# Moving the late attention loads and probability writes to another engine's queue, and re-ordering additions in a fused attention and feed-forward kernel

## The chip, the cores and the metric

The kernel runs on 1 core of a Trainium2 chip. Its engines each run one instruction stream in order: TensorE (PE, matmuls; PEld is its weight load), VectorE (DVE), ScalarE (ACT), GpSimd (POOL) and SyncE (SP, which here only issues DMA transfers). POOL and ACT can issue DMAs too. The metric is the time of one execution on the device, in microseconds (us); lower is better. "KB" is 1024 bytes.

## The reference

Attention with 4 batches, 8 heads, 768 positions and a head size of 64, in which a position sees 8 global keys and a local band of 96, with a slope per head for the distance; then a feed-forward layer 512 -> 2048 -> 512 with a leaky ReLU over the 3072 rows.

```python
scores = scale * np.matmul(q, k.transpose(0, 1, 3, 2))
is_global = pos[None, :] < int(n_global)
is_local = (rel >= 0) & (rel < int(n_local))
scores = scores - slopes[:, None, None] * dist
scores = np.where(is_global | is_local, scores, -1000000000.0)
a = np.exp(scores - np.max(scores, axis=-1, keepdims=True))
attn = np.matmul(a / (np.sum(a, axis=-1, keepdims=True) + 1e-09), v)
h = x @ w_in            # x: attn as 3072 rows of 512
return np.maximum(0.01 * h, h) @ w_out
```

All in float32, which the kernel reaches with products of a high and a low part (three matmuls for one).

## The kernel before, in words

**Attention** is cut into 48 units (24 blocks of 128 rows, two groups of four heads). A unit u goes through: loads of queries, keys and values (`qs`, `kr` in `load_qk`, L158 to L173; `vr` in `load_v`, L175 to L183), scores on PE (L200), biased scores and row maxima on DVE (`biased`, L214, into the buffer `pr`), exponentials on ACT (L229), sums and scaling on DVE (`sums`, L249 to L256), a transposition in 32x32 blocks on DVE (L259) that is completed by a trip through DRAM (`move`, L232: one DMA `via<-pr` out, L239, then four DMAs `pt<-via` back, L241), and at last the product with the values (`attn_v`, L333 and L345). There are two `pr` buffers, so unit u+2 can write its biased scores only once the `via` of unit u has left.

**Feed-forward** runs as 80 steps j over chunks of 3, 3, 3, 3 and 2 blocks of rows (`order`, L463): each step is 12 matmuls into `ps_h` (L1155 to L1157, `hidden`) and, for the step before, 9 or 6 into `ps_o` (L1176 to L1178, `project`). The attention of later rows is put between these steps: up to unit 21 by `event`, one unit at a time (two of them at j = 32 and 33, L836), and from unit PAIRS = 22 on by `visit`, two units at a time, at the steps listed in `VISITS` (L26). A visit t takes the values' product of units t-4 and t-3, the scores of t and t+1, loads for t+2 and t+3 (queries, keys) and for t-2 and t-1 (values). Its exponentials and sums are spread over the next two steps through the list `behind`. All of the loads, the `via` writes, the `pt` reads and the output rows are issued by SP, in one order; POOL issues only the results of attention to DRAM (`xd<-xo`, L363) and one reload (L576). SP's order in a visit is: `qs`, `kr`, `kr`, `vr`, `vr`, then `via` and four `pt` of the first unit, `via` and four `pt` of the second. A `pt` read waits until its `via` has landed.

**Strassen-like stage.** The last 10 blocks of rows (two super-blocks of 4 and 6) are computed after step 79 in 16 pairs of hidden columns, with 7 products a pair instead of 8 (`strassen`, L674). `prepare(n)` (L590), called at the steps j = 80 + n from n = -10 on, frees the attention's buffers, loads the blocks of x and makes their differences and splits; `make_sum` (L549) makes sums of weights on POOL, except `s3` of the pairs n + 2 < 8, which DVE makes (L756, L806). `prepare_next(i)` (L639) loads and subtracts blocks of the second super-block, in the pairs of the first. `add` (L701) reads a product from PSUM on DVE and then lets out the waiting low-part subtractions (`flush`, L509); `pin` and `keep_in_program_order` keep an instruction at its place in the order of the text; unpinned ones (the DMAs of `move`) are placed by the compiler's scheduler.

Of the kernel before, what the change touches and what calls it, by code (L numbers as in the profile page):

```python
# [18 lines left out]
P = 128  # L19
# [3 lines left out]
PAIRS = 22  # L23
HT = 384
SUPERS = [4, 6]
VISITS = [37, 39, 41, 43, 45, 48, 50, 52, 55, 57, 59, 62, 64, 67, 69]  # L26
RELOAD = 50
TB = 32
G = 8
# [3 lines left out]
KC = G + WIN + HALF  # L33
# [20 lines left out]
def fast_path(ctx, tc, qp, kp, vp, wi, wo, nvec, weights, nmall, out, B, H, S):  # L54
    nc = tc.nc
# [48 lines left out]
    def pin(ins):  # L104

        if pinned[0]:
            tc.keep_in_program_order(ins)
# [24 lines left out]
    def where(u):  # L132
        s, uu = divmod(u, NU)
        return s, uu, s % NB
# [23 lines left out]
    qs = {}  # L158

    def load_qk(u):  # L160
        s, uu, i = where(u)
        if uu == 0:
            qs[s] = raw.tile([P, 2 * NU, P], F32, tag="qkr", name="qs")
            pin(nc.sync.dma_start(out=qs[s], in_=qp[s]))
        k = raw.tile([P, 2, 2, KC], F32, name="kr")
        if i:
            pin(nc.sync.dma_start(out=k, in_=kp[s, uu]))
        elif u < BY_DVE:
            pin(nc.sync.dma_start(out=k[:, :, :, KC - P:], in_=kp[s, uu][:, :, :, KC - P:]))
        else:  # L170
            kd, ks = (x.rearrange("p a f (s x) -> p (a f s) x", s=2) for x in (k, kp[s, uu]))
            nc.sync.dma_start(out=kd[:, :, (KC - P) // 2:], in_=ks[:, :, (KC - P) // 2:])
        units[u] = dict(q=qs[s][:, 2 * uu:2 * uu + 2], k=k)  # L173

    def load_v(u):  # L175
        s, uu, i = where(u)
        if u > PAIRS and u % 4 == (PAIRS + 3) % 4:
            v = att.tile([P, 5, 2, D], F32, tag="pt", name="vr", bufs=1)
        else:
            v = raw.tile([P, 5, 2, D], F32, name="vr", bufs=3)  # L180
        g0 = 0 if i else 3
        pin(nc.sync.dma_start(out=v[:, g0:], in_=vp[s, uu][:, g0:]))
        units[u]["v"] = v  # L183

    def tall(u):
# [46 lines left out]
    def move(u, pr):  # L232


        pt = raw.tile([P, 4 * KW], F32, tag="stage", name="pt", bufs=STAGES)
        src, dst = blocks(u, pr), blocks(u, pt)
        n = src.shape[-1]
        via = dram.tile([4, TB, 4, 2 * n], F32, tag="via", name="via", bufs=3)
        nc.sync.dma_start(out=via.rearrange("b p c x -> (b p) c x"), in_=src.rearrange("p c j x -> p c (j x)"))  # L239
        for c in range(4):  # L240
            nc.sync.dma_start(out=dst[c * TB:(c + 1) * TB].rearrange("p b j x -> p b (j x)"),  # L241
                              in_=via[:, :, c].rearrange("b p x -> p b x"))
        units[u]["pt"] = pt
# [129 lines left out]
    def event(t, conv=()):  # L373
# [23 lines left out]
        if t + 2 < NUNIT:  # L397
            load_qk(t + 2)
# [107 lines left out]
    NP = NF // 2  # L506
    lows = []

    def flush():  # L509
        while lows:  # L510
            lows.pop(0)()
# [4 lines left out]
    late, here, blocks_x, dd = {}, {}, [{}, {}], {}  # L516

    def half_of(n):
        return SUPERS[n // NP] * P // 2

    def value(x):
        return x[1].bitcast(F32)
# [7 lines left out]
    def split_x(x, v=None):  # L530
        v = value(x) if v is None else v
        pin(nc.scalar.copy(out=x[0], in_=v))
        low(x[1], v, x[0])

    def spare():
        return pools["mem"].tile([P, 2, HT], F32, tag="diff", name="diff", bufs=2)

    def minus(out, in0, in1):
        pin(nc.vector.tensor_tensor(out=out, in0=in0, in1=in1, op=ALU.subtract))
        return out  # L540
# [8 lines left out]
    def make_sum(n, k, eng=nc.gpsimd):  # L549

        if n >= len(SUPERS) * NP:
            return
        b = blocks_of(n % NP)
        a11, a12, a21, a22 = ([x.bitcast(F32) for x in b[k]] for k in ("a11", "a12", "a21", "a22"))
        terms = dict(s1=(a21[0], (ALU.add, a22[0]), (ALU.add, a21[1]), (ALU.add, a22[1])),
                     s2=(here["s1"], (ALU.subtract, a11[0]), (ALU.subtract, a11[1])),
                     s3=(a11[0], (ALU.subtract, a21[0]), (ALU.add, a11[1]), (ALU.subtract, a21[1])),
                     s4=(a12[0], (ALU.subtract, here["s2"]), (ALU.add, a12[1])))[k]
        acc_ = terms[0]
        for op, t in terms[1:]:  # L560
            pin(eng.tensor_tensor(out=here[k], in0=acc_, in1=t, op=op))  # L561
            acc_ = here[k]
# [27 lines left out]
    def prepare(n):  # L590

        xa = blocks_x[0]
        if n == -10:
            early.close()
            pools["mem"] = mem = phase.enter_context(tc.tile_pool(name="late", bufs=1, side="right", reuse_waits="tile"))
            pools["ps"] = phase.enter_context(tc.tile_pool(name="ps_q", bufs=1, space=bass.MemoryType.PSUM, side="right", reuse_waits="tile"))
            late["x"] = x = mem.tile([P, 5 * 4 * HT], F32R, name="x")
            for m, k in enumerate(("b11", "t2", "b21", "t3", "t1", "t4", "b22")):
                cut(0, k, x, m * 2 * SUPERS[0] * P)
            for m, k in enumerate(("b21", "t3", "t1", "t4", "b22")):  # L600
                cut(1, k, x, m * 2 * SUPERS[1] * P)
            for k, to in (("b12", "t3"), ("b11", "b11"), ("b22", "b22"), ("b21", "b21")):
                load_x(0, k, value(xa[to]))
            for k in ("s1", "s2", "s3", "s4"):
                late[k] = [mem.tile([P, 2, P], F32R, name=k + x_) for x_ in "hl"]
                here[k] = mem.tile([P, 2, P], F32, name=k)
            for k in ("s1", "s2", "s3", "s4"):
                make_sum(0, k)
            band_holds(tc, fl, nvec, nmall)
        elif n == -9:  # L610
            band_holds_everywhere(tc, fl, pools["ps"].tile([P, HT], F32, tag="ps_p", name="ps_f")[0:1, 0:1], flag)
        elif n == -8:
            late["d1"] = minus(spare()[:, :, :half_of(0)], value(xa["t3"]), value(xa["b11"]))
            late["d2"] = minus(spare()[:, :, :half_of(0)], value(xa["b22"]), late["d1"])
        elif n == -7:
            split_x(xa["b11"])
            split_x(xa["t1"], late["d1"])
        elif n == -6:
            split_sum(0, "s2")
            split_sum(0, "s3")  # L620
            split_x(xa["t2"], late["d2"])
        elif n == -5:
            split_sum(0, "s1")
            split_sum(0, "s4")
            flush()
            for k in ("s1", "s2", "s3", "s4"):
                make_sum(1, k)
            late["d4"] = minus(spare()[:, :, :half_of(0)], late["d2"], value(xa["b21"]))
        elif n == -4:
            split_x(xa["t4"], late["d4"])  # L630
        elif n == -3:
            late["d3"] = minus(spare()[:, :, :half_of(0)], value(xa["b22"]), value(xa["t3"]))
            split_x(xa["b21"])
        elif n == -2:
            split_x(xa["t3"], late["d3"])
        elif n == -1:
            split_x(xa["b22"])
# [36 lines left out]
    def strassen():  # L674
# [26 lines left out]
        def add(name, in0, ps, op=ALU.add):  # L701
            t = (in0 if name is None else
                 (ffn if name == "t" else mem).tile([P, HT], F32, name=name, **(dict(bufs=2) if name == "u2" else {}))[:, :ps.shape[-1]])
            pin(nc.vector.tensor_tensor(out=t, in0=in0, in1=ps, op=op))  # L704
            flush()
            return t
# [30 lines left out]
        for n in range(last + 1):  # L737
# [14 lines left out]
            i, ht = n % NP, half_of(n)  # L752
            b = blocks_of(i)
            x, y = ((lambda bank=bank: bank()[:, :ht]) for bank in (banks[::-1] if n % 2 else banks))
            change = n == NP - 1
            sums_by = nc.vector if n + 2 < NP else nc.gpsimd  # L756
            gs = {}
            ps = x()
            product(n, b["a11"], "b11", ps)
# [32 lines left out]
            if change:  # L792
                fetch_next("t1")
            c22 = add("t", u3, ps)
            if change:
                split_x(blocks_x[1]["b21"])
            split_sum(n + 1, "s1")
# [5 lines left out]
            c21 = add(None, u3, ps2, ALU.subtract)  # L803
            for k in ("s1", "s2"):
                make_sum(n + 2, k)
            make_sum(n + 2, "s3", sums_by)  # L806
            if n == last - 1:
                gs[1, 0] = halves(c21, ht)
            gs[1, 1] = halves(c22, ht)
# [8 lines left out]
                gs[1, 0] = halves(c21, ht)  # L818
            if change:
                split_x(blocks_x[1]["t1"])  # L820
            if n < NP:
                prepare_next(i)
            rest = lambda gs=gs, c12=c12, ht=ht: gs.update({(0, 1): halves(c12, ht)})
            behind_(12)
            todo = [(lambda m=m, n=n, gs=gs: second(n, gs, m)) for m in range(2 * SUPERS[n // NP])]
# [6 lines left out]
    ev_at = {}  # L832
    for c in (1, 2):
        events = range(NU * first_step[c] + 2, NU * first_step[c + 1] + 2)
        ev_at.update(spread(events, range(1, half) if c == 1 else [24, 25, 27, 28, 30, 31]))
    ev_at.update({32: [20], 33: [21]})  # L836
    ev_at.update({j: [t] for j, t in zip(VISITS, range(PAIRS, NUNIT + 4, 2))})

    for t in range(2):
        load_qk(t)  # L840
# [424 lines left out]
```

## Time and profile before

| | us |
|---|---|
| median of 3 runs | 713.54 (710.51 to 715.38) |
| the profiled execution, its own time | 708.05 |
| span of the profiled execution | 706.5 |
| PE busy | 637.2 (90%) |
| DVE busy | 480.2 (68%) |
| ACT busy | 298.5 (42%) |
| POOL busy | 161.6 (23%) |
| mean granted TensorE clock | 0.965 |

The span runs from the first to the last instruction of the program. Busy shares are means over stages: the attention events take the first 206 us or so, the visits lie between 223 and 434 us, `prepare` between 435 and 467 us, the Strassen-like stage from 467 us on, its first super-block until about 573 us. A row of a timeline gives start, duration, engine, line, operation, tiles and, in brackets, how long the engine had been idle and what ended it. "q" behind an engine's name is its sequencer, as in SPq, which issues DMAs.

### The profile page before, as it was taken

The numbers are of one execution on the slowest core, as the hardware profiler recorded it, in microseconds if no ns is written. First come the engines' busy times: TensorE is split into PE (matmuls) and PEld (weight loads), VectorE is DVE, ScalarE is ACT, GpSimd is POOL, SyncE is SP. The second block draws the span as 40 slices with busy tenths as digits, with TensorE's granted clock in tenths as the row PEclk, the third lists the DMA queues.
The fourth block names the chain that finished last, engine by engine and source line by source line (L and its number), as shares of the span: only waits on it lengthen the run. The fifth ranks groups of instructions, "written<-read, shape, count | busy, mean of one in ns | idle before, by whom it ended". The sixth has DMA issues, their size and how long they took to land.

```text
span 706.5 us, 15386 instructions
## 1 busy us (share of the span) xinstructions
PE 637.2 (90%) x5836; PEld 554.7 (79%) x5836; DVE 480.2 (68%) x1319; ACT 298.5 (42%) x876; POOL 161.6 (23%) x220
## 2 busy tenths in 40 slices
PE   5799999999979978987969796989978979999996
PEld 4589898888868867876859785877857868888985
DVE  6988989866664765655665461687977876666743
ACT  6977745554433444443434341433233333223211
POOL 4213100000000000010000013343543655544500
PEclk9899999999999999988999898999999999999999
DMA  8975534226674557678666673020100300000002
GB/s 270 333 271 191 188 134 149 90 84 206 213 230 117 174 176 223 209 260 219 227 210 197 204 239 110 28 96 24 46 23 24 113 31 30 1 1 0 1 2 93
DMA packets 60321, 95.98 MB, mean 136 GB/s; under 512 B 10448, under 2 KB 33744, under 8 KB 60240
## 3 DMA queue, kind: packets, MB, share of 16 engines
q1 hardware_dynamic: 58800, 90.99, 39.8%
q0 software_dynamic: 1296, 3.67, 1.6%
q8 instruction: 48, 0.79, 0.5%
q14 instruction: 33, 0.27, 0.1%
q10 hardware_dynamic: 144, 0.26, 0.1%
HBM read 71.44 MB, written 23.46 MB: 134 GB/s over the span
## 4 chain that ended last, share of the span: by engine, by line
PE 59%; DVE 17%; DMA 10%; ACT 6%; issue 4%; SPq 2%; POOL 1%; ACTq 0%; DVEq 0%; POOLq 0%
PE ps_p L684 9%; PE ps_o L1178 7%; PE ps_o L1176 6%; PE ps_o L1177 6%; PE ps_h L1155 6%; PE ps_h L1157 5%; PE ps_h L1156 5%; DMA via<-pr 5%; DMA vr<-in_vp_dram 4%; PE ps_q L1177 2%; PE ps_q L1176 2%; PE ps_q L1178 2%; PE ps_v L345 2%; SPq L241 2%; DVE s L561 2%
## 5 line engine op out<-in xcount | busy, mean ns | idle before, releaser
L1176 PE MATMUL ps_o<-woh,gh 128*128 128x512 f32 x288 | 114.2, 396 | 3.7 <-ACT gh L1165 3.0
L1178 PE MATMUL ps_o<-woh,gl 128*128 128x512 f32 x288 | 114.5, 398 | 0.1
L1177 PE MATMUL ps_o<-wol,gh 128*128 128x512 f32 x288 | 113.5, 394 | 0.0
L1155 PE MATMUL ps_h<-xh,wih 128*128 128x384 f32 (+1 forms) x320 | 108.3, 338 | 0.1
L1156 PE MATMUL ps_h<-xl,wih 128*128 128x384 f32 (+1 forms) x320 | 104.5, 326 | 0.0
L1157 PE MATMUL ps_h<-xh,wil 128*128 128x384 f32 (+1 forms) x320 | 104.3, 326 | 0.0
L363 POOL DMA_DIRECT2D xd<-xo x24 | 17.7, 737 | 337.0 <-ACT xo L362 336.8
L229 ACT ACTIVATE pr<-pr,nmall 128x168 f32<-128x168 f32 (+1 forms) x192 | 80.3, 422 | 16.5 <-DVE nmall L214 16.5
L561 POOL TENSOR_TENSOR s<-s,wil 128x256 f32<-128x256 f32 x84 | 71.1, 846 | 6.6
L1160 DVE SCALAR_TENSOR_TENSOR t<-t 128x384 f32<-128x384 f32 (+1 forms) x80 | 46.8, 585 | 34.3 <-ACT t L1159 33.8
L1155 PEld LDWEIGHTS ps_h<-xh,wih 128*128 128x128 f32 x320 | 60.5, 189 | 8.4 <-issue 3.0
L1178 PEld LDWEIGHTS ps_o<-woh,gl 128*128 128x128 f32 x288 | 54.1, 188 | 14.5 <-DVE gl L1166 2.0
L1176 PEld LDWEIGHTS ps_o<-woh,gh 128*128 128x128 f32 x288 | 54.1, 188 | 13.0 <-ACT gh L1165 4.7
L1159 ACT COPY t<-ps_h 128x384 f32<-128x384 f32 (+1 forms) x80 | 36.2, 452 | 62.2 <-PE ps_h L1157 62.2
L1156 PEld LDWEIGHTS ps_h<-xl,wih 128*128 128x128 f32 x320 | 60.6, 190 | 2.2
L1157 PEld LDWEIGHTS ps_h<-xh,wil 128*128 128x128 f32 x320 | 60.4, 189 | 0.1
L1177 PEld LDWEIGHTS ps_o<-wol,gh 128*128 128x128 f32 x288 | 54.1, 188 | 8.1
L1165 ACT CAST gh<-t 128x384 fp32r<-128x384 f32 (+1 forms) x80 | 39.3, 491 | 49.1 <-DVE t L1160 48.4
L1166 DVE TENSOR_TENSOR gl<-t,gh 128x384 fp32r<-128x384 f32 (+1 forms) x80 | 42.4, 530 | 25.4 <-ACT gh L1165 22.9
L214 DVE CUSTOM_DVE_ANT_0 pr<-ps_v,nbw 128x168 f32<-128x168 f32 x88 | 24.0, 329 | 47.5 <-ACT xo L362 23.9
L704 DVE TENSOR_TENSOR u<-u,ps_p 128x256 f32<-128x256 f32 (+1 forms) x64 | 30.9, 482 | 36.3 <-PE ps_p L684 31.3
L697 ACT CAST gh<-u 128x256 fp32r<-128x256 f32 (+1 forms) x32 | 14.7, 460 | 72.8 <-DVE u L696 72.8
(177 smaller groups left out, 1328.6 us busy)
## 6 DMA issues: line engine op xcount, KB each, us to landing
kr<-in_kp_dram SPq DMA_DIRECT2D x40, 336.0 KB, 3.9
vr<-in_vp_dram SPq DMA_DIRECT2D x40, 320.0 KB, 5.0
via<-pr SPq DMA_DIRECT2D x30, 384.0 KB, 3.4
pt<-via SPq DMA_DIRECT2D x120, 96.0 KB, 2.4
wst<-in_wi_dram SPq DMA_DIRECT2D x16, 512.0 KB, 3.8
wst<-in_wo_dram SPq DMA_DIRECT2D x16, 512.0 KB, 3.7
qs<-in_qp_dram SPq DMA_DIRECT2D x24, 256.0 KB, 3.8
out_dram<-part SPq DMA_DIRECT2D x18, 256.0 KB, 2.2
```

What stands on the lines that cost most here:

```text
L229: pin(nc.scalar.activation(out=p, in_=p, func=AF.Exp, scale=-1.0, bias=nm[:, 2 * a + j:2 * a + j + 1], accum_out=sm[:, 2 * a + j:2 * a + j ...
L561: pin(eng.tensor_tensor(out=here[k], in0=acc_, in1=t, op=op))
L684: tc.keep_in_program_order(nc.tensor.matmul(ps, lhsT=w[x][:, m], rhs=x_[y][:, m], start=first and m == r == 0, stop=m == 1 and r == 2, ski ...
L1155: tc.keep_in_program_order(nc.tensor.matmul(ps, lhsT=wih[:, k, fs], rhs=xh[:, k, :CT], start=(k == 0), stop=False))
L1156: tc.keep_in_program_order(nc.tensor.matmul(ps, lhsT=wih[:, k, fs], rhs=xl[:, k, :CT], start=False, stop=False))
L1157: tc.keep_in_program_order(nc.tensor.matmul(ps, lhsT=wil[:, k, fs], rhs=xh[:, k, :CT], start=False, stop=(k == NK - 1)))
L1160: pin(nc.vector.scalar_tensor_tensor(out=t, in0=t, scalar=0.01, in1=t, op0=ALU.mult, op1=ALU.max))
L1165: pin(copy(out=gh, in_=t))
L1166: pin(nc.vector.tensor_tensor(out=gl, in0=t, in1=gh.bitcast(F32), op=ALU.subtract))
L1176: tc.keep_in_program_order(nc.tensor.matmul(o, lhsT=gh[:, ts_], rhs=woh[:, f, :], start=first, stop=False))
L1177: tc.keep_in_program_order(nc.tensor.matmul(o, lhsT=gh[:, ts_], rhs=wol[:, f, :], start=False, stop=False))
L1178: tc.keep_in_program_order(nc.tensor.matmul(o, lhsT=gl[:, ts_], rhs=woh[:, f, :], start=False, stop=last))
```

## The change

In words:

- Queries and keys of units from 24 on, and values of units from 23 on, are issued by POOL instead of SP. A key tile of a first block (i = 0) among them is loaded whole (336 KB instead of 256 KB).
- The `via` writes of units from 22 on are issued by POOL, at their place in the order of the text. The four `pt` reads stay on SP.
- The visits are at other steps, one or two later; the events 20 and 21 at j = 33 and 35 instead of 32 and 33.
- `prepare` begins at n = -8 instead of -10; what it did in ten steps it does in eight.
- In a pair of the first super-block, `prepare_next` comes behind the addition of the fifth product instead of behind the seventh, and DVE's `s3` sums come behind the pair's last activation, after a flush, instead of ahead of the sixth product's activation.

```diff
-VISITS = [37, 39, 41, 43, 45, 48, 50, 52, 55, 57, 59, 62, 64, 67, 69]
+VISITS = [38, 40, 42, 44, 46, 49, 51, 54, 56, 58, 60, 62, 65, 68, 71]
...
     def load_qk(u):
         s, uu, i = where(u)
+        queue = nc.gpsimd if u > PAIRS + 1 else nc.sync
...
-            pin(nc.sync.dma_start(out=qs[s], in_=qp[s]))
+            pin(queue.dma_start(out=qs[s], in_=qp[s]))
...
-        if i:
-            pin(nc.sync.dma_start(out=k, in_=kp[s, uu]))
+        if i or u > PAIRS + 1:
+            pin(queue.dma_start(out=k, in_=kp[s, uu]))
...
-        pin(nc.sync.dma_start(out=v[:, g0:], in_=vp[s, uu][:, g0:]))
+        pin((nc.gpsimd if u > PAIRS else nc.sync).dma_start(out=v[:, g0:], in_=vp[s, uu][:, g0:]))
...
-        nc.sync.dma_start(out=via.rearrange("b p c x -> (b p) c x"), in_=src.rearrange("p c j x -> p c (j x)"))
+        if u < PAIRS:
+            nc.sync.dma_start(out=via.rearrange("b p c x -> (b p) c x"), in_=src.rearrange("p c j x -> p c (j x)"))
+        else:
+            pin(nc.gpsimd.dma_start(out=via.rearrange("b p c x -> (b p) c x"), in_=src.rearrange("p c j x -> p c (j x)")))
...
-        if n == -10:
+        if n == -8:
             early.close()
...
-        elif n == -9:
+        elif n == -7:
             band_holds_everywhere(tc, fl, pools["ps"].tile([P, HT], F32, tag="ps_p", name="ps_f")[0:1, 0:1], flag)
-        elif n == -8:
             late["d1"] = minus(spare()[:, :, :half_of(0)], value(xa["t3"]), value(xa["b11"]))
             late["d2"] = minus(spare()[:, :, :half_of(0)], value(xa["b22"]), late["d1"])
-        elif n == -7:
             split_x(xa["b11"])
+        elif n == -6:
             split_x(xa["t1"], late["d1"])
...
             c22 = add("t", u3, ps)
+            if n < NP:
+                prepare_next(i)
...
             for k in ("s1", "s2"):
                 make_sum(n + 2, k)
-            make_sum(n + 2, "s3", sums_by)
+            if n + 2 >= NP:
+                make_sum(n + 2, "s3")
...
-            if n < NP:
-                prepare_next(i)
+            if n + 2 < NP:
+                flush()
+                make_sum(n + 2, "s3", nc.vector)
...
-    ev_at.update({32: [20], 33: [21]})
+    ev_at.update({33: [20], 35: [21]})
```

## Rows read from the trace of the kernel before

**Rows 1.** Waits of PE: who waited for whom; total us, times, longest.
```profile
PE ps_v L333 <- DMA vr<-in_vp_dram: 20.8, 5, 5.8
...
PE ps_v L333 <- issue: 6.1, 2, 3.9
...
PE ps_av L333 <- DMA pt<-via: 3.7, 4, 2.8
```
**Rows 2.** Timeline of SP from 357 to 365 us, issues with their duration.
```profile
357.38 0.39 SPq L239 DMA_DIRECT2D via<-pr  x1
360.67 1.73 SPq L241 DMA_DIRECT2D pt<-via  x4
362.44 0.43 SPq L164 DMA_DIRECT2D qs<-in_qp_dram  x1
362.96 0.85 SPq L167 DMA_DIRECT2D kr<-in_kp_dram  x2
363.87 0.90 SPq L182 DMA_DIRECT2D vr<-in_vp_dram  x2
```
**Rows 3.** Timeline of PE, the beginnings of two visits.
```profile
353.65 0.49 PE L333 MATMUL ps_v<-pt,vr 64*64 64x128 f32 x5
...
370.33 0.82 PE L333 MATMUL ps_v<-pt,vr 64*64 64x128 f32 x8 [4.87 <-DMA vr<-in_vp_dram]
```
**Rows 4.** Timeline of DVE between these two visits.
```profile
355.20 0.98 DVE L259 STREAM_TRANSPOSE pr<-pr 128x768 f32<-128x768 f32 x1
...
360.81 0.33 DVE L214 CUSTOM_DVE_ANT_0 pr<-ps_v,nbw 128x168 f32<-128x168 f32 x1 [3.31 <-DMA via<-pr]
```
**Rows 5.** Windows: busy us (instructions) by engine, granted clock, DMA share, GB/s.
```profile
223.30:431.10 207.80, 178.20 (x2021) 156.09 (x2020) 120.38 (x469) 86.09 (x306) 16.99 (x23) 0.92 0.66 207
437.00:467.00 30.00, 29.19 (x187) 25.80 (x186) 20.60 (x37) 12.23 (x31) 16.23 (x19) 1.00 0.12 36
467.00:574.00 107.00, 92.70 (x548) 77.62 (x547) 85.17 (x167) 35.62 (x93) 49.25 (x60) 1.00 0.17 54
```
**Rows 6.** Windows around a visit without a wait and one after a wait.
```profile
342.20:345.00 2.80, 2.80 (x114) 2.55 (x113) 0.77 (x3) 0.38 (x2) 0.00 (x0) 1.00 0.52 166
...
306.40:311.60 5.20, 5.20 (x113) 4.74 (x113) 1.06 (x6) 0.37 (x1) 0.25 (x1) 0.50 0.66 241
```
**Rows 7.** Sum of six such windows, the visits at 260, 275, 306, 325, 370, 403 us.
```profile
sum 26.80, PE 26.69 PEld 24.74 DVE 5.13 ACT 2.24 POOL 0.84; mean PE 4.45 PEld 4.12 DVE 0.85 ACT 0.37 POOL 0.14
```
**Rows 8.** DMA issues: KB each, median us from issue to landing.
```profile
kr<-in_kp_dram SPq DMA_DIRECT2D x40, 336.0 KB, 3.9
vr<-in_vp_dram SPq DMA_DIRECT2D x40, 320.0 KB, 5.0
via<-pr SPq DMA_DIRECT2D x30, 384.0 KB, 3.4
pt<-via SPq DMA_DIRECT2D x120, 96.0 KB, 2.4
...
qs<-in_qp_dram SPq DMA_DIRECT2D x24, 256.0 KB, 3.8
...
xd<-xo POOLq DMA_DIRECT2D x24, 128.0 KB, 2.9
```
**Rows 9.** DMA issues of POOL at L363: duration in ns, least, median, most.
```profile
L363 POOL DMA_DIRECT2D xd<-xo x24: 708/726/944, 263.2 to 435.0; - x24
```
**Rows 10.** Window with the highest DMA share among 10 us stretches of the visits.
```profile
300.00:310.00 10.00, 6.68 (x111) 5.96 (x113) 5.98 (x18) 2.27 (x8) 0.00 (x0) 0.77 0.90 295
```
**Rows 11.** Waits of PE, the two longest of the Strassen-like stage.
```profile
PE ps_p L684 <- ACT u L761: 6.3, 7, 1.8
PE ps_p L684 <- DVE u L704: 5.0, 6, 1.9
```
**Rows 12.** Timeline of DVE in one pair: s3 sums, activation, addition of c12.
```profile
485.73 0.41 DVE L561 TENSOR_TENSOR s<-wih 128x256 f32<-128x256 f32 x1
486.17 1.73 DVE L561 TENSOR_TENSOR s<-s,wil 128x256 f32<-128x256 f32 x2
...
488.70 0.41 DVE L704 TENSOR_TENSOR u<-u,ps_p 128x256 f32<-128x256 f32 x1
```
**Rows 13.** Timeline of PE in the same pair: the product that waited.
```profile
489.16 0.51 PE L684 MATMUL ps_p<-x,s2h 128*128 128x256 f32 x2 [0.55 <-DVE u L704]
```

More of the change, by code (lines that the diff above doesn't have):

```diff
@@ L161, in load_qk @@
         s, uu, i = where(u)
+        queue = nc.gpsimd if u > PAIRS + 1 else nc.sync
         if uu == 0:
             qs[s] = raw.tile([P, 2 * NU, P], F32, tag="qkr", name="qs")
-            pin(nc.sync.dma_start(out=qs[s], in_=qp[s]))
+            pin(queue.dma_start(out=qs[s], in_=qp[s]))
         k = raw.tile([P, 2, 2, KC], F32, name="kr")
-        if i:
-            pin(nc.sync.dma_start(out=k, in_=kp[s, uu]))
+        if i or u > PAIRS + 1:
+            pin(queue.dma_start(out=k, in_=kp[s, uu]))
         elif u < BY_DVE:
-            pin(nc.sync.dma_start(out=k[:, :, :, KC - P:], in_=kp[s, uu][:, :, :, KC - P:]))
+            pin(queue.dma_start(out=k[:, :, :, KC - P:], in_=kp[s, uu][:, :, :, KC - P:]))
         else:
@@ L609, in prepare @@
             band_holds(tc, fl, nvec, nmall)
-        elif n == -9:
+        elif n == -7:
             band_holds_everywhere(tc, fl, pools["ps"].tile([P, HT], F32, tag="ps_p", name="ps_f")[0:1, 0:1], flag)
-        elif n == -8:
             late["d1"] = minus(spare()[:, :, :half_of(0)], value(xa["t3"]), value(xa["b11"]))
             late["d2"] = minus(spare()[:, :, :half_of(0)], value(xa["b22"]), late["d1"])
-        elif n == -7:
             split_x(xa["b11"])
+        elif n == -6:
             split_x(xa["t1"], late["d1"])
-        elif n == -6:
+            split_x(xa["t2"], late["d2"])
+        elif n == -5:
             split_sum(0, "s2")
             split_sum(0, "s3")
-            split_x(xa["t2"], late["d2"])
-        elif n == -5:
+            late["d4"] = minus(spare()[:, :, :half_of(0)], late["d2"], value(xa["b21"]))
+        elif n == -4:
             split_sum(0, "s1")
@@ L627, in prepare @@
                 make_sum(1, k)
-            late["d4"] = minus(spare()[:, :, :half_of(0)], late["d2"], value(xa["b21"]))
-        elif n == -4:
             split_x(xa["t4"], late["d4"])
@@ L755, in strassen @@
             change = n == NP - 1
-            sums_by = nc.vector if n + 2 < NP else nc.gpsimd
             gs = {}
```

## The prediction

> **What bounds the kernel now.** I read the page first: PE is busy for 90% of the span, so the time to be won is PE's idle time and its time at the low clock. The waits of PE, longest first, say where that lies: 20.8 us in which a visit's first value product waited for `vr`, and 6.1 us put down to "issue" at the same instruction, where `vr` had also only just landed; a further 3.7 us belong to the events before the visits, which wait for `pt` [rows 1]. All of the visits together last 207.8 us, of which PE works 178.2 [rows 5].
>
> The timeline of SP says why `vr` is late. The visit at 353.65 starts without a wait and the next one waits 4.87 us [rows 3]. Its loads come from SP in the order of the text, behind the second `via` of the visit before and its four `pt`, which cannot go before that `via` has landed. So SP starts the `via` at 357.38, the `pt` at 360.67, `qs` at 362.44, `kr` at 362.96 and `vr` at 363.87 [rows 2]. DVE had finished the transposition that this `via` sends at 356.18 (355.20 plus 0.98) [rows 4]. SP is a queue with waits in it, and the loads of the next visit stand at its end.
>
> A wait costs twice. [...] Six visits after waits take 26.80 us together, where six undisturbed ones would take 16.8: 10.0 us more [rows 7]. So the visits' loads cost 26.9 us of idling and 10.0 us of low clock.
>
> **The change part by part.**
>
> *Loads to POOL.* SP loses five issues a visit, POOL gains them, ahead of its two `xo` writes. One of POOL's issues takes 0.73 us [rows 9] against about 0.43 on SP [rows 2]. Behind them on POOL stand the `xo` writes; nobody on PE waits for these.
>
> *`via` to POOL.* Its wait for the transposition moves to POOL, and what is queued behind it there is the next visit's loads. For the visit at 370.33: POOL could send the `via` at 356.18; `qs`, `kr`, `kr` and the first `vr` follow, five issues of 0.73 = 3.65 us, so the second `vr` starts at 359.8 instead of 364.35 (363.87 plus half of 0.90). That is 4.5 us earlier, against a wait of 4.87: 0.4 us is left. The wait of SP for the landing stays with `pt`, which are used two visits later, so that wait is hidden by a visit of 11.45 us (353.65 less 342.20 [rows 3, 6]). The `pr` buffers also come free sooner; DVE's wait of 3.31 us for them [rows 4] lies beside PE's work and I cost it at nothing: PE works a step ahead of DVE, and if that cover were gone it would cost up to 3.3 us a visit.
>
> *What limits next: the DMA engines.* A full visit moves 256 + 2 x 336 + 2 x 320 + 2 x 384 + 8 x 96 + 2 x 128 = 3360 KB = 3.44 MB [rows 8]. The visits' stage moves 207 GB/s at a share of 0.66 [rows 5], so 314 GB/s at a full share and 11.0 us a visit. A visit two steps behind the last has 11.45 us. The highest share seen is 0.90 [rows 10]; at that the visit takes 12.2 us, 0.7 more than PE needs. Eight of the new gaps are so tight (42 to 44, 44 to 46, 49 to 51, four from 54 to 62, and 65 to 68, whose three steps are short). I put 0.4 + 0.7 us of wait on each, 9 us, and 1 us for clock: **+10 us left over**. Bounds: 0, if the burst of loads spreads out; +34 (2.6 us of wait and the whole 10.0 / 6 = 1.7 us of low clock at each of eight), if the share stays near 0.78, halfway between the stage's mean and its highest. I stay near the low end, because three-step gaps between the tight ones let the queues empty.
>
> [...]
>
> *Events 20 and 21 later.* The 3.7 us of waiting for `pt` [rows 1] goes, since the event before now has one more step of lead and the next two more. Bounds 0 and -3.7; I take **-3.7**.
>
> *`prepare` in eight steps.* No work is added. From 437 to 467 us DVE is busy for 20.6 of 30 us and PE for 29.2 [rows 5]. In eight steps of 2.8 us, an estimate from this window's pace (30 us for ten and a little), DVE has about 19 us to do in 22.4, a share of 0.85, beside POOL's sums. In the next stage, where DVE is busy for 85.17 of 107 us, PE idles for 14.3 (107 less 92.70), 13% [rows 5]. The same share of 22.4 us is 3; I take **+2.5**, bounds 0 and +6 (two steps' worth).
>
> *Order in the pairs.* DVE's `s3` sums (0.41 + 1.73 us) stand now ahead of the addition at 488.70 that lets PE's next product go, which waited 0.55 us [rows 12, 13]. They move behind it and then stand ahead of the next pair's first addition. So a wait is not removed, it moves to a place with more or less the same slack. The block subtractions and splits of `prepare_next` move away from the end of the pair, where ACT's copy stands behind them; they are part of the 6.3 us there. All of both waits is 11.3 us [rows 11]. Bounds: -11 to +4 (the 2.1 us of sums not covered in two pairs of six); I take **-2**, nearer to nothing, because DVE's busy time does not change and is 80% of the stage.
>
> **The sum.** Against the profiled execution's own 708.05 us: -26.9 (idle) -10.0 (clock) -3.7 (events) +10 (left over) -2 (pairs) +2.5 (`prepare`) = 678.0. The runs' median, 713.54, lies 5.5 us above that execution, so I predict **683**.
>
> **The rivals.**
>
> *A, the forecast*: the queue was the limit, the DMA engines take up some 10 us of it. 674 to 694. Chance 0.57.
>
> *B, the DMA engines become the bound*: the burst of five loads and the `pt` reads now meet, the share stays near 0.78, +34 us is left over instead of +10: 707; halfway there 695. For it: 3.44 MB in 11.45 us is 300 GB/s, more than the 295 of the busiest stretch [rows 10]. Against it: the mean over the visits is 207 [rows 5], so there is room between. 694 to 708. Chance 0.20.
>
> *E, nothing is left over*, and the pairs gain 6 to 8 as well: 708.05 - 40.6 - 6 + 2.5 + 5.5 = 669. Chance 0.10.
>
> *D, the change does not do what it says*: the loads stand behind a `via` on POOL as they did on SP, and DVE's transpositions come so late that the loads go no earlier. Then they would have to end near 362 instead of 356 [rows 2, 4]; nothing delays them by that much, since DVE is busy for 120 of 208 us [rows 5]. 709 to 716. Chance 0.07.
>
> *C, slower: POOL's issues become the bound.* POOL issues nine DMAs in a full visit, 6.6 us at 0.73. [...] Against it: the 24 issues at L363 took 0.94 us at most [rows 9]. [...] Chance 0.06. [...]
>
> **How the numbers follow.** A measurement of this kernel tells about 1% from no change: 706.4 to 720.7. The range, 667 to 707, holds A, E but for its lowest part, and nearly all of B; above it are D, C and the end of B (0.16), below it 0.03. Faster by over 1%: A, E and 0.17 of B, 0.84. Within 1%: D and 0.03 of B, 0.10. Slower: C, 0.06.
>
> **What would show it.** Right: SP issues only `pt` and output rows between 240 us and the end of the visits; the waits for `vr` fall from 26.9 us to under 12; the clock of the visits' stage rises from 0.92 to 0.97 or more; its DMA rate rises from 207 to about 240 GB/s; the visits' stage with its 32 to 33 steps is some 30 us shorter. The leftover is right if the remaining waits stand at the tight gaps and DMA's share there is near 0.9. `prepare` is right if PE idles 1 to 4 us in the last eight steps, with DVE named. The pairs are right if the waits for the c12 addition go and others, at the fourth product, come. Wrong: issues of POOL well over 0.73 us; loads that start no earlier than 6 us after a visit's scores; a DMA share of 0.8 or less with late loads.

## The result, and the profile after

The changed kernel takes **679.47 us** (median of 4 runs, 675.21 to 680.32), the kernel before 714.46 beside it (4 runs, 710.51 to 716.68): ratio 0.9504, 95% interval 0.9445 to 0.9563. It is faster, and 3.5 us below the 683 of the forecast. The profiled execution took 679.73 us. The one of before, 708.05 us, was among the fastest of its kernel, so the two traces account for 28.3 of the 35.0 us between the medians.

Three windows of the changed kernel come first: the visits, from their first value product to the first Strassen-like product; the same and the feed-forward step ahead of them; and about the last eight steps. The columns are those of [rows 5]. Line numbers differ by a few between the kernels (the value product is L333 before and L337 after).

```profile
224.20:440.00 215.80, 201.20 (x2281) 172.96 (x2281) 138.92 (x504) 98.52 (x337) 81.06 (x130) 1.00 0.68 207
...
219.94:440.00 220.06, 205.46 (x2302) 176.54 (x2301) 140.13 (x506) 99.51 (x339) 81.06 (x130) 1.00 0.67 205
...
417.00:440.00 23.00, 21.94 (x136) 18.78 (x136) 17.18 (x31) 9.74 (x25) 13.56 (x16) 1.00 0.15 46
```

The visits of the kernel before, between the same two instructions as in the first window:

```profile
223.31:466.77 243.46, 213.02 (x2301) 187.26 (x2301) 141.29 (x506) 99.27 (x339) 35.88 (x45) 0.92 0.58 182
```

The stretch of the visits is 27.7 us shorter (215.80 against 243.46). Not all of that is won, because the visits now begin one feed-forward step later: a step of 21 matmuls and 4.3 us has moved from this stretch to the one ahead of it. The window that begins at 219.94 holds the same matmuls as the one of before, and by it the visits are 23.4 us shorter. PE's idle time falls from 30.4 us (243.46 less 213.02) to 14.6, and its busy time by 7.6 us, at a granted clock of 1.00 where it was 0.92. What stands after the visits lasts 231.2 us instead of 233.2. What stands ahead of them, without the step that was added, takes 219.9 instead of 223.3.

The waits of PE (total us, times, longest) answer to [rows 1, 11]:

```profile
PE ps_v L337 <- DMA pt<-via: 8.1, 10, 2.6
...
PE ps_p L686 <- DVE u L706: 6.8, 7, 1.1
PE ps_o L1181 <- ACT gh L1170: 3.7, 4, 1.5
...
PE ps_v L337 <- issue: 2.5, 2, 1.2
PE ps_p L686 <- ACT u L762: 1.8, 2, 1.3
```

No wait for `vr` is left by name. The two put down to "issue" are `vr` all the same: the products start at 273.55 and 358.62 us, and a `vr` had landed 0.09 us before each. What PE now waits for in the visits is mostly `pt`.

POOL's timeline (start, duration, in brackets the idle time before and its releaser) answers to [rows 2]:

```profile
276.97 0.56 POOL L243 DMA_DIRECT2D via<-pr  x1 [3.31 <-DVE pr L263]
277.55 0.54 POOL L165 DMA_DIRECT2D qs<-in_qp_dram  x1
278.35 1.07 POOL L168 DMA_DIRECT2D kr<-in_kp_dram  x2 [0.26 <-issue]
279.44 1.07 POOL L183 DMA_DIRECT2D vr<-in_vp_dram  x2
282.03 0.73 POOL L367 DMA_DIRECT2D xd<-xo  x1 [1.52 <-ACT t L1164]
```

The `via` begins 0.40 us after its transposition, which ended at 276.57, and the second `vr` 3.0 us after the `via` (279.98). In the trace of before the second `via` of a visit began 1.0 to 5.0 us after its transposition in 12 of 13 visits (3.0 us on average over the 13), and the loads stood behind its landing.

The longest wait for `pt` shows the new chain, on SP and then on PE:

```profile
292.84 2.58 SPq L245 DMA_DIRECT2D pt<-via  x4
295.52 1.68 SPq L507 DMA_DIRECT2D out_dram<-part  x3
297.30 1.93 SPq L245 DMA_DIRECT2D pt<-via  x3
```

```profile
306.06 0.40 PE L337 MATMUL ps_v<-pt,vr 64*64 64x128 f32 x2 [2.58 <-DMA pt<-via]
306.88 0.33 PE L337 MATMUL ps_v<-pt,vr 64*64 64x128 f32 x3 [0.41 <-DMA pt<-via]
```

The unit's transposition ends at 290.75 and its `via` lands at 294.04, but the reads begin at 297.30, behind three rows of output, and land 6 to 8 us later, with the next visit's loads and those rows already under way. In the 10 us before PE goes on, the DMA engines have a share of 1.00:

```profile
296.06:306.06 10.00, 7.43 (x72) 6.25 (x71) 6.73 (x18) 3.68 (x14) 2.53 (x5) 1.00 1.00 323
```

The median time from issue to landing of a `pt` has risen from 2.4 us [rows 8] to 5.1.

### The profile page after: what moved, and what is told of

Read it like the earlier page. It is cut to its first block, busy times and chain, and to the rows that moved or that the text cites. A ratio compares the mean times of both kernels' runs of the same rounds, so it can differ in the third digit from the quotient of the medians.

```text
span 678.2 us, 15414 instructions
## 1 busy us (share of the span) xinstructions
PE 630.6 (93%) x5836; PEld 543.3 (80%) x5836; DVE 478.1 (71%) x1319; ACT 298.1 (44%) x876; POOL 209.2 (31%) x307
## 2 busy tenths in 40 slices
DMA packets 51041, 96.31 MB, mean 142 GB/s; under 512 B 6352, under 2 KB 29136, under 8 KB 50960
## 4 chain that ended last, share of the span: by engine, by line
PE 56%; DVE 20%; DMA 9%; ACT 6%; issue 6%; POOL 2%; SPq 0%; ACTq 0%; DVEq 0%; POOLq 0%
PE ps_p L686 9%; PE ps_o L1183 6%; PE ps_o L1181 6%; PE ps_o L1182 6%; PE ps_h L1160 6%; DMA pt<-via 5%; PE ps_h L1162 5%; PE ps_h L1161 5%; DMA via<-pr 4%; DVE gl L518 2%; PE ps_q L1183 2%; PE ps_q L1181 2%; PE ps_q L1182 2%; DVE pr L260 2%; DVE s L565 2%
## 5 line engine op out<-in xcount | busy, mean ns | idle before, releaser
L230 ACT ACTIVATE pr<-pr,nmall 128x168 f32<-128x168 f32 (+1 forms) x192 | 80.4, 422 | 18.6 <-DVE nmall L215 18.2
L165 POOL DMA_DIRECT2D qs<-in_qp_dram x12 | 6.8, 564 | 131.7 <-PE ps_av L201 131.4
```

Source lines behind the costliest of these rows:

```text
L230: pin(nc.scalar.activation(out=p, in_=p, func=AF.Exp, scale=-1.0, bias=nm[:, 2 * a + j:2 * a + j + 1], accum_out=sm[:, 2 * a + j:2 * a + j ...
```

## The experiments

Each kernel below was timed beside the kernel before, on the same chip. The table splits the profiled executions: *front* is the time to the first value product of a visit, *visits* from there to the first Strassen-like product, *idle* PE's idle time in the visits (length less PE busy), *clock* the granted clock there, *rest* the time from there to PE's last instruction.

| kernel | median us | ratio (95%) | front | visits | idle | clock | rest |
|---|---|---|---|---|---|---|---|
| before | 714.46 | | 223.3 | 243.5 | 30.4 | 0.92 | 233.2 |
| after | 679.47 | 0.950 (0.945 to 0.956) | 224.2 | 215.8 | 14.6 | 1.00 | 231.2 |
| e1 queues only | 686.82 | 0.962 (0.957 to 0.968) | 226.3 | 217.9 | 13.4 | 1.00 | 233.3 |
| e2 order only | 706.72 | 0.990 (0.986 to 0.993) | 221.4 | 242.4 | 36.0 | 0.94 | 231.3 |
| e3 loads only | 707.56 | 0.990 (0.985 to 0.994) | 222.6 | 247.6 | 37.7 | 0.92 | 231.4 |
| e4 via only | 683.64 | 0.957 (0.952 to 0.962) | 225.1 | 218.2 | 18.3 | 0.98 | 231.2 |
| e5 pairs undone | 679.72 | 0.955 (0.947 to 0.963) | 222.5 | 215.0 | 11.4 | 0.98 | 233.6 |
| e6 scratch size | 678.59 | 0.949 (0.944 to 0.953) | 223.2 | 215.2 | 11.4 | 0.98 | 231.6 |
| e7 sums earlier | 673.45 | 0.945 (0.937 to 0.953) | 222.1 | 212.4 | 10.2 | 0.99 | 231.3 |
| e8 more bytes | 684.58 | 0.957 (0.953 to 0.961) | 222.9 | 219.7 | 15.3 | 0.98 | 231.4 |
| e10 pt on POOL | 677.86 | 0.951 (0.944 to 0.959) | 222.5 | 216.2 | 13.4 | 0.98 | 231.3 |
| e11 third pr | 701.12 | 0.984 (0.977 to 0.991) | 237.5 | 222.4 | 18.6 | 0.97 | 231.3 |
| e12 sums and rows | 673.38 | 0.940 (0.936 to 0.944) | 222.3 | 214.1 | 11.0 | 0.98 | 231.4 |
| e13 pt on POOL, sums | 675.96 | 0.944 (0.941 to 0.947) | 223.8 | 217.1 | 14.9 | 0.98 | 231.4 |

The visits of before and e1 hold the feed-forward step of 4.3 us that all the others have in the front, so stretches of these two are compared with each other, and the others among themselves. The front differs by 3 to 4 us between kernels whose work there is the same (e11 aside), so effects of 1 to 3 us are read from the stretch that they belong to.

**e1 and e2: the two halves of the change.** The kernel before with the new queues alone, and the changed kernel with loads and `via` back on SP.

```diff
 e1: the kernel before, with the edits of load_qk, load_v and move alone
 e2: the changed kernel, without them
```

> The kernel before with the queue edits alone (loads and via on GpSimd); steps of the visits, prepare and the pairs as before. Theory (SP's one order made the loads late): the vr waits of 26.9 us and the 10 us at the low clock go, the 3.7 us of the events stay: 683 to 688 us. Rival (the new places of the visits give the time): 700 us or more.

> The changed kernel with all loads and via back on SP; new visit steps, prepare in eight steps and the new order in the pairs stay. Theory: only the events' 3.7 us and about 2 us of the pairs are won, 704 to 711 us, and the waits for vr stay above 15 us. Rival (the new places): 695 us or less.

Both came out as expected: 686.82 and 706.72 us. In the visits the queues bring 25.5 us (e1 against before) or 26.6 us (the changed kernel against e2), and e2 still waits 19.8 us for `vr` by name, at a clock of 0.94. The order brings 2.0 us in the rest, and nothing in the visits: for the same products they are some 2 us longer with it (220.06 against e1's 217.93). In e1 the waits for `pt` at `ps_av`, which went with the later events, are still there (4.1 us).

**e3 and e4: the two halves of the queues.** Loads alone on POOL, and `via` alone on POOL.

```diff
 e3, in move():
-        if u < PAIRS:
-            nc.sync.dma_start(out=via..., in_=src...)
-        else:
-            pin(nc.gpsimd.dma_start(out=via..., in_=src...))
+        nc.sync.dma_start(out=via..., in_=src...)
 e4, in load_qk() and load_v(): nc.sync for every load, as before
```

> The changed kernel with the via writes back on SP, loads on GpSimd. Theory: the loads are what was late, so within 5 us of the changed kernel: 678 to 685 us; the second via of a visit waits for four pt, so pt come 1 to 2 us later than in the changed kernel. Rival (via is what matters): 700 us or more.

> The changed kernel with the loads back on SP, via on GpSimd. Theory: the loads still stand behind eight pt that wait for the landing of via, so the vr waits stay above 12 us: 698 to 710 us. Rival (via is what matters): 690 us or less.

Both theories missed, and both times lie where the rival, that `via` is what matters, had put them. With the loads alone on POOL the kernel takes 707.56 us, some 22 more than the end of what was expected and no less than e2: all of the queues' gain is lost. With `via` alone there it takes 683.64, 14 less than expected, and its visits are only 2.4 us longer than the changed kernel's, though PE still waits for `vr` (8.2 us by name and 6.3 by "issue"). So the prediction's account, in which the loads' new queue was the gain, is not enough. Where e3 loses stands in the waits of its DVE and its PE:

```profile
DVE pr L215 <- DMA via<-pr: 59.2, 9, 8.9
```

```profile
PE ps_o L1178 <- ACT gh L1167: 37.6, 9, 7.2
```

No `vr` is late in it and no `pt`. PE stops at `ps_o`, for the hidden layer's activation, and one such place can be followed through four timelines (DVE, SP, POOL, PE):

```profile
282.18 0.98 DVE L260 STREAM_TRANSPOSE pr<-pr 128x768 f32<-128x768 f32 x1
...
292.03 0.33 DVE L215 CUSTOM_DVE_ANT_0 pr<-ps_v,nbw 128x168 f32<-128x168 f32 x1 [7.88 <-DMA via<-pr]
...
293.05 0.55 DVE L1162 SCALAR_TENSOR_TENSOR t<-t 128x384 f32<-128x384 f32 x1
```

```profile
281.70 2.73 SPq L242 DMA_DIRECT2D pt<-via  x4
284.52 0.38 SPq L240 DMA_DIRECT2D via<-pr  x1
```

```profile
282.91 1.16 POOL L168 DMA_DIRECT2D kr<-in_kp_dram  x2 [14.02 <-PE ps_v L201]
284.09 1.06 POOL L183 DMA_DIRECT2D vr<-in_vp_dram  x2
```

```profile
294.20 0.80 PE L1178 MATMUL ps_o<-woh,gh 128*128 128x512 f32 x1 [4.66 <-ACT gh L1167]
```

The transposition ends at 283.16. SP is at the reads of the first unit then and issues the second `via` at 284.52, 1.4 us late. Meanwhile POOL, which has no issue that waits for one of SP's, has begun both `kr` and the first `vr`. The `via` is under way together with them and lands 7.35 us after its issue. DVE's next biased scores need that `pr` buffer, and the hidden layer's addition stands behind them in DVE's order (293.05), so PE stops for 4.66 us, and its next product takes 0.80 us, where a product of the same line takes 0.40 in the changed kernel at 301.78. The pattern holds over the whole trace: in eight of the 13 visits `kr` loads were in flight when the second `via` began, and it took 5.2 to 9.4 us (7.2 on average); in the other five 2.6 to 3.8 us (3.1). In the changed kernel the second `via` stands ahead of the loads on POOL's own queue and takes 2.7 to 4.7 us.

**e11: is it the buffer?** e3 with a third `pr` buffer; the room for it comes from letting the first units' `dg` share `xo`'s two buffers.

```diff
-    prs = [att.tile([P, 4 * KW], F32, name="pr", bufs=2) for _ in range(2)]
+    prs = [att.tile([P, 4 * KW], F32, name="pr", bufs=3) for _ in range(3)]
...
-        pr = prs[u % 2]
+        pr = prs[u % 3]
...
-        dg = att.tile([P, 4, HALF], F32, name="dg", bufs=1)
+        dg = att.tile([P, 4, HALF], F32, tag="work", name="dg", bufs=2)
```

> The changed kernel with via back on SP (707.6 us) and a third buffer for the probabilities pr (room made by letting the first units' dg share the two buffers of xo). Theory (with via on SP the loss is that pr comes free late, VectorE waits for it ahead of the hidden layer's additions and TensorE stops at ps_o): VectorE's waits for via fall from 59 us to below 10, TensorE's stops at ps_o for gh from 37.6 to below 10; what then may show is the late landing of pt, so 680 to 694 us. Rival (the late via itself is what costs, through pt, with VectorE's wait only its shadow): pt's waits take the place of gh's, 700 to 710 us.

The total, 701.12 us, is the rival's, but the stretches say otherwise. The front is 14.9 us longer than in e3; that lies ahead of the visits, where `dg` now shares `xo`'s buffers. PE's waits for `dg` account for only 2.2 us of it (10.9 us at `ps_tr`, 8.7 in e3), and what else lengthens the front stays open. In the visits, which the question was about, 25.2 of the 31.8 us between e3 and the changed kernel come back. DVE's wait for `via` is gone from its list, the stop at `ps_o` falls from 37.6 to 1.5 us, and what takes its place is the late `pt`:

```profile
237.50:459.85 222.35, 203.79 (x2281) 177.26 (x2280) 140.21 (x504) 97.26 (x337) 66.80 (x104) 0.97 0.64 201
```

```profile
PE ps_v L334 <- DMA pt<-via: 17.2, 14, 3.9
```

So most of e3's loss in the visits ran through the `pr` buffer. The visits are still 6.6 us longer than the changed kernel's, with longer waits for `pt`.

**e10: or is it the reads back?** Loads and `via` on SP as before, in the new order, and the `pt` reads on POOL: nothing that SP issues waits for a landing.

```diff
-            nc.sync.dma_start(out=dst[c * TB:(c + 1) * TB]..., in_=via[:, :, c]...)
+            (nc.sync if u < PAIRS else nc.gpsimd).dma_start(out=dst[c * TB:(c + 1) * TB]..., in_=via[:, :, c]...)
```

> The new visits and pairs, the loads and the move to DRAM (via) on SP as before, but the four reads back (pt) of each unit from the 22nd on are begun by GpSimd. Theory (what cost the kernel before its time is that the second via of a visit, and the loads, stand on SP's queue behind four reads that wait for the first via's landing): nothing on SP waits for a landing any more, so 678 to 688 us, the waits of TensorE for vr below 9 us between 190 and 440 us, VectorE's waits for via below 20 us. Rival (it is which engine begins the big transfers that counts, so via and the loads must leave SP themselves): as with the new order alone, 702 to 710 us.

677.86 us, as the theory had it, and no different from the changed kernel. Among its waits of PE `vr` is the longer of the two that are left in the visits, as the forecast had meant:

```profile
PE ps_v L333 <- DMA vr<-in_vp_dram: 6.6, 4, 3.5
...
PE ps_v L333 <- DMA pt<-via: 2.3, 2, 1.3
```

Here it matters little, then, which engine begins the big transfers (677.86 us, and 679.47 in the changed kernel). Two things matter: `via` and loads don't stand behind `pt`, which waits for a landing, and the second `via` goes ahead of the loads. The kernel before breaks the first rule for both, and e4 for the loads alone. e3 breaks it for `via`, by 0.7 us on average, and breaks the second rule in eight visits. The changed kernel and e10 keep both. Whether one queue would do, with both `via` of a visit issued ahead of all the reads, was not tried.

**e5: the pairs.** The old order inside the pairs.

```diff
-            if n < NP:
-                prepare_next(i)
...
-            if n + 2 >= NP:
-                make_sum(n + 2, "s3")
+            make_sum(n + 2, "s3", nc.vector if n + 2 < NP else nc.gpsimd)
...
-            if n + 2 < NP:
-                flush()
-                make_sum(n + 2, "s3", nc.vector)
+            if n < NP:
+                prepare_next(i)
```

> The changed kernel with the old order of the s3 additions and of the next blocks' preparation inside the pairs. Theory (the new order in the pairs is worth the 2 us that the idle time of the first super-block shows): 681 to 682.5 us, TensorE's waits for VectorE's addition to c12 back at about 5 us. Rival (nothing, what is saved there is paid at the fourth product): 679 to 680.5 us.

The median, 679.72, is the rival's number. The stretch that the edit changes shows the theory's: the rest lasts 233.6 us instead of 231.2, and the wait for DVE's addition is back at 5.1 us. The visits and the front of this execution were 0.8 and 1.7 us shorter, which hides it. The runs' medians don't confirm the 2.4 us, but the table does: in the three kernels with the old order inside the pairs (before, e1, e5) the rest lasts 233.2 to 233.6 us, in the other eleven 231.2 to 231.6.

The instructions of e5's visits are those of the changed kernel, and so are those of e6 further down. `pt` is waited for less in both, where the changed kernel shows 8.1 us; so e5 tells how far such waits move from one execution to the next (e5 first, then e6):

```profile
PE ps_v L337 <- DMA pt<-via: 4.0, 5, 1.4
...
PE ps_v L337 <- DMA pt<-via: 4.8, 8, 1.3
```

**e8: are the DMA engines the bound?** One more copy of each unit's keys, DRAM to DRAM, that nobody reads.

```diff
+        if u > PAIRS + 1:
+            extra = dram.tile([P, 2, 2, KC], F32, name="extra", bufs=3)
+            pin(nc.sync.dma_start(out=extra, in_=kp[s, uu]))
```

> The changed kernel with one transfer more for each unit of the visits: SP copies the unit's keys once more, from DRAM to DRAM, into a buffer that nobody reads (672 KB a visit on top of 3.44 MB). Theory (the 16 DMA engines are the bound of the close visits, as the sum's term for what is left over says): 672 KB at the full share's 3.2 us per MB are 2.1 us a visit, of which 0.45 us is spare, so some 1.7 us in each of 8 close visits: 690 to 697 us. Rival (what is left over is the length of the chain transposition, via, pt in its order on the queues, and the engines still have room): 679 to 683 us.

684.58 us: 5.1 more than the changed kernel, between the two. The visits move 238 GB/s at a share of 0.75 and are 3.9 us longer for 8.3 MB more (104.57 against 96.31 MB in all), 0.5 us per MB where a full share would need 3.2 (an estimate from the 207 GB/s at a share of 0.66 in [rows 5]):

```profile
222.90:442.63 219.73, 204.41 (x2280) 177.02 (x2280) 139.53 (x504) 97.91 (x337) 80.86 (x130) 0.98 0.75 238
```

Over the visits as a whole the engines still had room. In bursts they had little: in the changed kernel their share is 0.89 to 1.00 in the 10 us before the end of each of the five waits above 1 us. So the added bytes cost far less than the theory's price. That bytes add to the waits only where they lie ahead of a `pt` or `vr` in such a burst fits this, but no run separates it.

**e7 and e12: a shorter chain.** The second unit's sums one place earlier (e7), and besides the output rows of the visits issued by ACT (e12).

```diff
 e7 and e12:
-            ... (exps(t + 1, [1]), sums(t)), lambda: None, lambda: sums(t + 1)])
+            ... (exps(t + 1, [1]), sums(t)), lambda: sums(t + 1), lambda: None])
 e12:
-            nc.sync.dma_start(out=out[r0:r0 + P, :], in_=ob)
+            (nc.scalar if c > 1 else nc.sync).dma_start(out=out[r0:r0 + P, :], in_=ob)
```

> The changed kernel with the second unit's sums, scaling and transposition one place earlier in the list of work behind the hidden layer's activations, so that its via begins some 3 us earlier. Theory (what is left over of the idle time in the visits is pt, late by up to 2.6 us at the end of a chain transposition, via, pt): TensorE's waits for pt fall from 8.1 to below 3 us, and the time to 673 to 677 us. Rival (VectorE's scaling then stands ahead of the hidden layer's additions, or waits for the exponentials, and TensorE stops at ps_o for gh): 679 to 686 us.

> The changed kernel with the second unit's sums one place earlier (673.5 us alone) and the rows of output that are written during the visits begun by ScalarE in place of SP, where three of them stood ahead of reads back of pt. Theory (pt's waits that are left come partly from what stands ahead of its reads on SP): TensorE's waits for pt 4.3 to below 2.5 us, 670 to 673 us. Rival (ScalarE's issues stand ahead of its exponentials and activations, and cost what they save): 673 to 677 us, waits for gh up.

e7 takes 673.45 us (671.52 to 679.11) and beats both kernels by median; its interval against before, 0.937 to 0.953, overlaps that of the changed kernel, so by this run the 6 us between the two are likely rather than certain. The visits are 3.4 us shorter than the changed kernel's, and 2.6 and 2.8 us shorter than e5's and e6's. The waits for `pt` do not fall to below 3 us, and are no lower than in e5, where the sums stand at their old place:

```profile
PE ps_v L337 <- DMA pt<-via: 4.3, 5, 1.5
```

e12's 673.38 us is no different from e7's; its interval, 0.936 to 0.944, lies just below the changed kernel's 0.9445 to 0.9563, and that bears out the gain of the edit that both have. That it comes from an earlier `pt` is not shown. The waits for `pt` fall further, to 2.8 us, but those put down to "issue" at the same product rise from 2.5 to 4.9, and no gain shows from moving the output rows.

**e6: the holds ahead of `xo`.** In the changed kernel 15 of the 24 `xo` writes were issued 0.33 us after an earlier transfer of GpSimd's had landed. e6 is the changed kernel with one number of the program raised.

```diff
-    nc = bacc.Bacc("TRN2", target_bir_lowering=False, num_devices=1, dynamic_dma_scratch_size=1024)
+    nc = bacc.Bacc("TRN2", target_bir_lowering=False, num_devices=1, dynamic_dma_scratch_size=1984)
```

> [...]

678.59 us, 0.9 less than the changed kernel. On POOL's timeline the two `xo` writes now follow the loads at once, where the changed kernel held the first until 282.03 and the second until 286.36:

```profile
277.21 1.07 POOL L168 DMA_DIRECT2D kr<-in_kp_dram  x2 [1.47 <-PE ps_v L201]
278.27 1.06 POOL L183 DMA_DIRECT2D vr<-in_vp_dram  x2
279.35 1.44 POOL L367 DMA_DIRECT2D xd<-xo  x2
```

**e13: both gains together.** e10 with the sums of e7.

> The new visits and pairs, loads and via on SP as before, the reads back of pt begun by GpSimd (677.9 us alone), and the second unit's sums one place earlier. Theory (a via that begins earlier lands pt earlier whichever queue the reads are on, and the two gains add): TensorE's waits for pt below 1.5 us, time 670 to 674 us, the best of all. Rival (what is left here is vr, late on SP behind via, 6.6 us, and an earlier via does nothing for it): vr's waits stay and the time is 675 to 679 us.

675.96 us (673.39 to 680.64), the rival's: `vr` is still waited for (4.8 us in 4 places). The time lies between e7's and e10's and can't be told from either, so it is not shown that the gains add. e7 and e12 have the lowest medians of these.

## Why the prediction was right, and where it was not

**The size held, term by term.** For the visits the terms come to -26.9 - 10.0 + 10 + 2.5 = -24.4 us; for the same products they are 23.4 us shorter (243.46 less 220.06). The events' -3.7 shows in the front: 3.4 us. The pairs' -2 shows in the rest: 2.0 us. The whole sum was 678.0 us for the profiled execution, which took 679.73. The +5.5 us from there to the median was wrong: it assumed that the changed kernel's profiled execution would be among the fastest of its kernel too, and it was 0.3 above the median.

**Loads and `via` on POOL: right as a whole, priced at the wrong part.** The step "five issues of 0.73 ... the second `vr` starts at 359.8" put the gain on the loads. The order it describes, transposition, `via`, loads, is the one in the trace, and the issues took 0.54 us, less than 0.73. But e3 has the loads' new queue without that order and gains nothing in the visits (247.6 us, where e2 takes 242.4), while e4 has the loads still on SP and keeps 24.2 of the 26.6 us between e2 and the changed kernel. The decisive part is that the second `via` doesn't wait behind `pt` for the first one's landing and goes ahead of the loads.

**"That wait is hidden by a visit of 11.45 us": the step that failed.** It priced `pt` at the latency of before, 2.4 us; in the changed kernel the median is 5.1, and the chain of transposition, `via` and reads shown above ran from 290.75 to 306.74 us, past the start of its visit at 302.57. `pt` costs 8.1 us in ten waits there.

**The 9 us of wait left over: right in size and place, wrong in what is waited for.** 10.6 us were measured (8.1 + 2.5); e5 and e6, with the same visits, show 7.0 and 8.4. 9.2 of the 10.6 us stand at the gaps that the forecast called tight, with a DMA share of 0.89 to 1.00 ahead of the long ones, so these two signs came true. But the term was meant for `vr`, and `pt` is most of it. That the number fits a wait for something else is luck. And full engines were not the bound of every close visit, as e8's 0.5 us per MB shows.

**DVE's wait for `pr`, costed at nothing: right, and only because of the cover named there.** In the changed kernel it is 17.1 us in 7 places, and PE's stops for `gh` come to 3.7. In e3 the cover is gone: 59.2 and 37.6 us, up to 8.9 at a place, more than the "3.3 us a visit" of the bound, because a wait's length was taken from a trace in which no loads were under way ahead of the second `via`.

**The clock: -10 and +1 forecast, 7.6 us measured.** That much less is PE's busy time for the same products, and 8.45 us less in e1; the visits' clock is 1.00 in both.

**The events: right.** The 3.7 us of `pt` at `ps_av` are gone; e1 shows that the later events did it.

**`prepare` in eight steps: +2.5 forecast, about nothing measured.** PE idles 1.06 us in the last 23 us of the visits, against 0.81 in the 30 us of before [rows 5], and the releaser is ACT's `gh`. DVE's share there is 0.75 (17.18 of 23), not 0.85; a share carried over from the next stage, where the waits come from the pairs' own order, was no price for it.

**The pairs: -2 forecast, -2.0 measured in the rest.** The waits for the addition to c12 are gone but for one of 0.51 us, and a wait of 1.05 us has come at the fourth product of six pairs, as forecast, because the sums now stand ahead of that addition. DVE and PE in one of them, against [rows 12, 13]:

```profile
474.62 0.96 DVE L565 TENSOR_TENSOR s<-wih 128x256 f32<-128x256 f32 x1
475.62 1.30 DVE L565 TENSOR_TENSOR s<-s,wil 128x256 f32<-128x256 f32 x2
476.84 0.41 DVE L706 TENSOR_TENSOR u<-u,ps_p 128x256 f32<-128x256 f32 x1
```

```profile
477.31 0.50 PE L686 MATMUL ps_p<-x,s3h 128*128 128x256 f32 x2 [1.05 <-DVE u L706]
```

What was won is the copy by ACT: its waits fall from 6.3 us [rows 11] to 1.8.

**The rivals.** B, the DMA engines as the bound, fell with the visits' length and with e8. C, slower by POOL's issues, fell with their duration (ns, least, median, most):

```profile
L183 POOL DMA_DIRECT2D vr<-in_vp_dram x25: 537/539/553, 227.8 to 402.8; - x25
```

The longest of POOL's issues in the changed kernel took 0.78 us (777 ns, at L165).

## What to carry to other kernels

Look on each DMA queue for an issue that waits for a landing, and for what stands behind it: give either the waiting issues or those behind them another queue; here it mattered little which (677.86 and 679.47 us). Once queues are split, check the order across them: a transfer that frees a buffer has to begin before the loads that would be under way beside it (in e3 `via` took 7.2 us on average with `kr` loads in flight at its beginning, and 3.1 without). A DMA's latency read from the trace before is a price only as long as the same transfers lie ahead of it (here the `pt` went from 2.4 to 5.1 us). And before two stretches are compared, count the instructions in them: an edit can move work across the cut.

## What was not expected of the hardware

In 15 of 24 cases in the changed kernel GpSimd issued `xo` 0.33 us after an earlier `via` or `kr` of its own had landed (282.03 after 281.70, 286.36 after 286.03), where nothing in the program makes it wait for that landing. In each of the 15 cases four or five of GpSimd's transfers were still under way. With `dynamic_dma_scratch_size` at 1984 instead of 1024 (e6) the `xo` writes at 279.35 and 294.78 us follow the loads at once, both times two within 1.44 us. Why the number has this effect was not shown. The time differs by 0.9 us, less than the runs of one kernel do.
